# A layer of attention and MLP on one core: a constant by memset, and magnitudes of weights as sums on ScalarE

## The chip, the core and the metric

The kernel runs on one core of a Trainium2 chip. The core has TensorE (PE, with its weight loads as PEld), VectorE (DVE), ScalarE (ACT), GpSimd (POOL) and SyncE (SP), which here issues all transfers. Each engine works through its own instructions in a fixed order and waits where a semaphore isn't yet up, so whatever stands behind a waiting instruction waits too. The metric is device time in microseconds for one execution; lower is better.

## The reference

For x of 2048 rows by 512, with 32 heads of 16 and an MLP of width 1792:

```python
xn = _layernorm(x)
qkv = (xn @ wqkv)                         # wqkv 512 x 1536
scores = einsum("bhqd,bhkd->bhqk", q, k) * 16 ** -0.5
o = einsum("bhqk,bhkd->bhqd", softmax(scores), v)
A = o @ wo                                # wo 512 x 512
h = gelu(xn @ w1 + b1)                    # w1 512 x 1792, tanh form
B = h @ w2 + b2                           # w2 1792 x 512
return x + A + B
```

## The kernel before, in words

**Numbers in two halves.** TensorE works in 16-bit floats. Each operand is split into a high and a low half, and a product is the sum of three (high by high, high by low, low by high). Weights are divided first by a power of two near their magnitude, so that the halves keep their range. That magnitude is measured on the chip: `absmax` (L728) reduces a chunk of weights to one value per partition on VectorE, and `scales` (L123) turns the values into one power of two per tensor by a transposition, a maximum, a product that spreads it to all partitions, and a mask on the bits. `fac` is the power, `inv` its inverse. `gs` (L954) holds four factors made from them.

**Stages.** 1. A prelude: `stats` normalises the rows of x, four tiles of 128 rows at a time (a block; the second half of each later block on ScalarE, in two passes over `xs`, L783 and L784), `transpose_x` transposes them to `xt`, `project` computes q and k of the first eight heads, `v_proj` computes v for one tile of 128 rows. q and k go through DRAM (`qk_d`) and come back as *stacks* (`kst`, `qst`): for a pair of heads 128 partitions, of which 48 per head hold the halves, two more rows per head hold the row maxima on the q side against a constant 1024 (`MROW`) on the k side, and the others hold zero. 2. The loop of `unit`s: 512 units for eight groups of four heads, each unit with scores for four heads (`s_half`, row maxima `mt` by VectorE at L260), exponentials of an earlier unit (`e_half`, ScalarE at L305), products with v (`v_half`) and a share of other matrix products on the same TensorE order (`dense`): first the projections of the remaining heads, then the MLP, then the output projection. 3. A tail.

In the prelude `tile_and_unit` runs four times per block: one tile of v beside the first sixteen units' scores. Their maxima are taken by VectorE as in the loop.

**The weights of the MLP.** `measure` (L829) goes over 16 chunks of 128 x 1024 values of w1, w2 and wo, each in two halves; `MEASURE` (L33) says how many halves follow each tile of the prelude: 0, 1 and 2 in blocks 1 to 3, 3 in the last four units. That is 24 halves; the other 8 are taken in the loop, one per unit, where `prepare` (L962) begins with `yield from ms`. Then `prepare` computes the factors and splits the chunks, which are loaded a second time (`every` holds the list twice), on GpSimd, in steps that are paid out at 2500 ns a unit. Chunks stand in three buffers named `wch`.

**The constant of the stacks.** `clear` (L82) sets each of the 32 stacks to zero on GpSimd and copies two rows of 1024 into each k stack per head by a transfer of 2 KB from `ones_row`, 16 transfers for each of the two sets: L88, 32 in all.

**Order.** Up to L1015 a scheduler chooses the order on each engine by its own estimates of times, so a change in one place can move many instructions of the prelude. From L1015 on (`manual_schedule`) the order is that of the code.

Of the kernel before, what the change touches and what calls it, by code (L numbers as in the profile page):

```python
# [1 line left out]

# [6 lines left out]
F32 = mybir.dt.float32  # L9
F16 = mybir.dt.float16  # L10
I32 = mybir.dt.int32
AF = mybir.ActivationFunctionType
ALU = mybir.AluOpType
AX = mybir.AxisListType
# [3 lines left out]
P = 128  # L18
# [11 lines left out]
VW = DH + 1  # L30
LEAD = 19
FAST, MEAN, SLOW = (4, 4), (3, 4), (3, 3)
MEASURE = (3, 0, 1, 2)  # L33
HALF = 1300
POOL_NS = 2500
TAIL = 5
# [4 lines left out]
GELU_C = 0.7978845608028654  # L41
GELU_A = 0.044715
MROW = 1024.0
W = 2 * P


@with_exitstack
def layer_kernel(ctx: ExitStack, tc: tile.TileContext, x, wqkv, wo, w1, b1, w2, b2, out):
    nc = tc.nc
# [3 lines left out]
    def pool(stack, name, bufs=1, space=None, side=None):  # L53
# [3 lines left out]
    const = pool(ctx, "const")  # L57
    work = pool(ctx, "work")
# [13 lines left out]

    ident = const.tile([P, P], F32, name="ident")
    make_identity(nc, ident)
    ones_row = const.tile([2, P], F16, name="ones_row")
    nc.vector.memset(ones_row, MROW)


    kst, qst = ([[[const.tile([P, QB], F16, name=f"{x}st{i}_{p}_{b}") for b in range(NQB)] for p in range(2)]
                 for i in range(2)] for x in "kq")  # L80

    def clear(i):  # L82
        for b in range(NQB):
            for p in range(2):
                for st in (kst[i][p][b], qst[i][p][b]):
                    nc.gpsimd.memset(st.bitcast(F32), 0.0)
                for a in range(2):
                    nc.sync.dma_start(kst[i][p][b][64 * a + 62:64 * a + 64, :].rearrange("r (b n) -> r b n", n=P),  # L88
                                      ones_row.unsqueeze(1).to_broadcast([2, 4, P]))

    vv = const.tile([P, NT, H * VW + 15], F32, name="vv")
    nc.gpsimd.memset(vv[:, :, 0:H * VW].rearrange("p t (h e) -> p t h e", e=VW)[:, :, :, DH], 1.0)
# [66 lines left out]
    def given(engine, ns):  # L159
        backlog[engine] += ns  # L160
# [102 lines left out]
    def s_end(u):  # L263
# [10 lines left out]
        def store():  # L274
# [433 lines left out]
    with ExitStack() as st1:  # L708
# [10 lines left out]
        def chunk(src):  # L719
            wf = ph.tile([P, 4 * W], F32, name="wch", bufs=3)  # L720
            v = wf.rearrange("p (a b) -> p a b", b=src.shape[2])
# [6 lines left out]
        def absmax(dst, v):  # L728
            nc.vector.tensor_reduce(dst, v, axis=AX.XY if len(v.shape) == 3 else AX.X, op=ALU.max,  # L729
                                    apply_absolute_value=True)  # L730
            given("dve", 600)
# [4 lines left out]
        wov = wo.rearrange("(c p) n -> p c n", p=P)  # L736
        every = [w1v[:, :, i * W:(i + 1) * W] for i in range(7)]
        every = every + [w2v[:, 2 * i:2 * i + 2, :] for i in range(7)] + [wov[:, 0:2, :], wov[:, 2:4, :]]
        every = every + every
        amx = work.tile([P, 16, 2], F32, name="amx")  # L740
        fac1 = []

        def fetch(k):
# [10 lines left out]
        loads = []  # L754
        wvf = [chunk(wvv[:, :, i * W:(i + 1) * W]) for i in range(2)]
        wvh = [ph.tile([P, NC, D], F16, name="wvh", tag="wsp", bufs=3) for _ in range(2)]
        fac_v, ready_w = [], {}
# [53 lines left out]
        def prep_v():  # L811
# [9 lines left out]
            for i in range(2):  # L821
                cs = slice(i * W, (i + 1) * W)
                split(wvh[0][:, :, cs], wvh[1][:, :, cs], wvf[i], inv[:, 0:1])

        def some(gen, n):
            for _ in range(n):
                next(gen, None)

        def measure():  # L829

            for n in range(16):
                v = fetch(n)
                for k in range(2):
                    absmax(amx[:, n, k:k + 1], v[:, 2 * k:2 * k + 2, :] if n < 7 else v[:, k, :])
                    yield

        ms = measure()

# [57 lines left out]
        for sb in range(1, NQB):  # L896
# [15 lines left out]
            for j in range(4):  # L912
                tile_and_unit(4 * sb - 4 + j)
                some(ms, MEASURE[sb])
                if sb == 1:
# [7 lines left out]
        for j in range(4):  # L923
            some(pq, 2)
            tile_and_unit(NT - 4 + j)
            some(ms, MEASURE[0])
        run(pq)
# [26 lines left out]
        gs = const.tile([P, 4], F32, name="gs")  # L954
# [6 lines left out]

        def prepare():  # L962
            yield from ms
            am = work.tile([P, 10], F32, name="am_all")
            nc.vector.tensor_reduce(am[:, 0:7], amx[:, 0:7, :], axis=AX.X, op=ALU.max)
            nc.vector.tensor_reduce(am[:, 7:8], b1_s, axis=AX.X, op=ALU.max, apply_absolute_value=True)
            nc.vector.tensor_reduce(am[:, 8:9], amx[:, 7:14, :], axis=AX.XY, op=ALU.max)
            nc.vector.tensor_reduce(am[:, 9:10], amx[:, 14:16, :], axis=AX.XY, op=ALU.max)
            box = []
            yield  # L970
            yield from scales(am, 10, sbank, box)
            inv, fac = box
            fac1.append(fac)

            nc.vector.reduce_max(gs[:, 0:1], fac[:, 0:8], axis=AX.X)
            nc.vector.tensor_tensor(gs[:, 3:4], fac_v[0][:, 0:1], fac[:, 9:10], op=ALU.mult)
            yield
            nc.vector.reciprocal(gs[:, 1:2], gs[:, 0:1])
            nc.vector.tensor_tensor(gs[:, 2:3], gs[:, 0:1], fac[:, 8:9], op=ALU.mult)
            yield  # L980
            nc.vector.tensor_scalar_mul(gs[:, 1:2], gs[:, 1:2], 0.5)
            ended = [True]
            for n in range(16):
                v = fetch(16 + n)
                while not ended[0]:
                    yield
                ended[0] = False

                def then(wh=None, n=n):
                    ended[0] = True  # L990
                    later(2, lambda: put(wh, n), True)
# [256 lines left out]
```

## Time and profile before

| What | Value |
|---|---|
| median of 3 runs | 1513.81 us (1510.95 to 1516.05) |
| profiled execution | 1513.79 us, its span 1512.0 us |
| busy: TensorE, VectorE, ScalarE, GpSimd | 1489.9, 1405.0, 1244.0, 663.7 us |
| prelude: first products of q and k; second block of x transposed from | 15.97 us; 23.65 us |
| prelude: first four units' v products; next four; third block's projection | 31.82 to 47.81 us; 56.75 to 71.96 us; to 77.8 us |
| table load on ScalarE, first exponentials | 120.56 us, 1.28 us long |
| last unit's scores | about 1450 us |

A row of the profile's groups reads: line, engine, operation, tile written <- tiles read, shape, count, then busy time and mean ns of one, then idle time before it and what ended that. A row of a timeline begins with start and length in us, and ends with the count of merged instructions and, in brackets, the idle time before and its releaser. A row of windows gives a stretch, its length, busy time and count of each engine, the granted TensorE clock, the share of the transfer engines and GB/s. The matmuls' ends are modelled, so TensorE can read as fully busy while its products are spaced apart.

### The profile page before, as it was taken

How to read it: one execution, taken by the hardware profiler on the slowest of the kernel's cores; microseconds unless marked ns; L12 is line 12 of the kernel's file. 1: busy time of each engine (PE TensorE's matmuls, PEld its weight loads, DVE VectorE, ACT ScalarE, POOL GpSimd, SP SyncE). 2: the span in 40 equal slices, each digit the busy share in tenths (PEclk: the TensorE clock that was granted, in tenths of full speed). 3: DMA queues.
4: the chain of work that ended last, by engine and by line, in shares of the span. 5: the costliest groups of instructions: out<-in, count | busy, mean ns of one | idle time of the engine just before them, and what ended most of it. 6: DMA issues, size and time to landing. Idle time of an engine off the chain costs nothing.

```text
span 1512.0 us, 86779 instructions
## 1 busy us (share of the span) xinstructions
PE 1489.9 (99%) x39407; PEld 822.7 (54%) x39407; DVE 1405.0 (93%) x2368; ACT 1244.0 (82%) x2317; POOL 663.7 (44%) x685
## 2 busy tenths in 40 slices
PE   8999999999999999999999999999999999999998
PEld 4434555555555555555555555555555555555553
DVE  7899999999999999999999999999999999999933
ACT  4326788889998888999888899998889998888885
POOL 4113598637772111777411158761216785211110
PEclk9999999999999999999999999999999999999998
DMA  6454477632222201131011211122102201112422
GB/s 199 132 160 148 148 218 228 195 106 81 67 78 57 70 27 35 44 84 50 22 50 42 65 41 43 36 78 64 34 18 62 79 27 29 49 54 60 131 65 97
DMA packets 113673, 123.75 MB, mean 82 GB/s; under 512 B 24988, under 2 KB 85276, under 8 KB 113304
## 3 DMA queue, kind: packets, MB, share of 16 engines
q1 hardware_dynamic: 113304, 118.21, 25.9%
q8 instruction: 308, 5.05, 1.4%
q14 instruction: 61, 0.50, 0.1%
HBM read 80.61 MB, written 37.34 MB: 78 GB/s over the span
## 4 chain that ended last, share of the span: by engine, by line
PE 81%; DVE 16%; issue 1%; DMA 1%; ACT 1%; POOL 0%; SPq 0%; ACTq 0%; POOLq 0%
PE pV L169 24%; PE pD L169 20%; PE pT L169 17%; PE pS L169 17%; DVE mt L260 14%; PE pT L438 1%; PE pD L438 1%; DVE amx L729 1%; PE pT L531 1%; PE pV L531 0%; DMA wq<-in_A_wqkv_dram 0%; DMA wch<-in_B_w_dram 0%; PE pT L799 0%; PE pS L438 0%; POOL xt L804 0%
## 5 line engine op out<-in xcount | busy, mean ns | idle before, releaser
L260 DVE TENSOR_REDUCE mt<-pS 128x1 f32<-128x512 f32 x2048 | 1304.7, 684 | 41.8 <-PE pS L169 25.9
L305 ACT ACTIVATE pe<-pT 128x512 f32<-128x512 f32 x2048 | 1112.3, 598 | 172.4 <-PE pS L169 82.0
L169 PE MATMUL pV<-pe,vv 64*32 64x512 f32 x8192 | 1076.5, 595 | 0.1
L169 PE MATMUL pT<-qst,kst 64*32 64x512 f16 x8192 | 719.5, 378 | 1.4 <-ACT pe L305 1.2
L169 PE MATMUL pS<-kst,qst 62*32 62x512 f16 x8192 | 624.8, 379 | 6.4 <-DVE mt L260 4.9
L169 PEld LDWEIGHTS <-kst 64*32 64x32 f16 x8192 | 289.4, 91 | 191.8 <-issue 94.2
L169 PEld LDWEIGHTS <-qst 62*32 62x32 f16 x8192 | 274.3, 92 | 206.0 <-issue 60.6
L169 PE MATMUL pD<-w_s,g 64*32 64x512 f16 x5376 | 364.6, 376 | 0.0
L169 PE MATMUL pD<-xb,wc 64*32 64x512 f16 x5376 | 361.1, 377 | 0.0
L169 PEld LDWEIGHTS pV<-pe,vv 64*32 64x32 f32 x8192 | 181.5, 105 | 88.4 <-PE pV L169 4.7
L1090 POOL TENSOR_TENSOR xa<-xa,yt 128x512 f32<-128x512 f32 x16 | 20.5, 1279 | 302.9 <-ACT yt L1088 302.9
L169 PEld LDWEIGHTS <-wc 64*32 64x32 f16 x5376 | 117.0, 91 | 42.7 <-issue 0.5
L169 PEld LDWEIGHTS <-g 64*32 64x32 f16 x5376 | 112.3, 91 | 45.6
L169 PE MATMUL pD<-xt,wqk_h 64*32 64x512 f16 x2016 | 135.9, 380 | 0.6 <-issue 0.4
L361 POOL TENSOR_TENSOR osb<-osb,rb 128x512 f32<-128x512 f32 x31 | 39.9, 1286 | 158.9 <-DMA rb<-den_d 120.3
L1045 POOL TENSOR_TENSOR t<-hh 128x512 f32<-128x512 f32 x56 | 58.3, 1041 | 86.5 <-ACT hh L1065 85.4
L1047 POOL TENSOR_TENSOR t<-t,hh 128x512 f32<-128x512 f32 x56 | 71.9, 1285 | 4.7
L1040 POOL TENSOR_TENSOR t<-t,hh 128x512 f32<-128x512 f32 x56 | 71.9, 1283 | 4.7
L1042 POOL TENSOR_TENSOR g<-t,g 128x512 f16<-128x512 f32 x56 | 65.2, 1165 | 4.7
L1039 POOL TENSOR_SCALAR t<-t,gs 128x512 f32<-128x512 f32 x56 | 39.0, 696 | 49.7 <-ACT t L1034 49.3
L169 PEld LDWEIGHTS <-wqk_h 64*32 64x32 f16 x2016 | 48.5, 92 | 21.5 <-issue 5.4
L169 PE MATMUL pD<-wo_s,oc 64*32 64x512 f16 x828 | 54.5, 378 | 0.0
(141 smaller groups left out, 868.9 us busy)
## 6 DMA issues: line engine op xcount, KB each, us to landing
wch<-in_B_w_dram SPq DMA_DIRECT2D x28, 512.0 KB
wc<-w_d SPq DMA_DIRECT2D x56, 256.0 KB
qk_d<-stg SPq DMA_DIRECT2D x32, 256.0 KB
rb<-den_d SPq DMA_DIRECT2D x124, 64.0 KB
w_d<-wsp SPq DMA_DIRECT2D x28, 256.0 KB
kst<-qk_d SPq DMA_DIRECT2D x128, 48.0 KB
qst<-qk_d SPq DMA_DIRECT2D x128, 48.0 KB
xs<-in_A_x_dram SPq DMA_DIRECT2D x16, 256.0 KB
```

The lines of the kernel that those rows point to most:

```text
L169: p = nc.tensor.matmul(*args, **kw)
L260: nc.vector.reduce_max(mt_of[t][:, n, qt, kb:kb + 1], s, axis=AX.X)
L305: nc.scalar.activation(pe, st, AF.Exp, scale=scale_of[g // 2])
L361: pooled((1280, lambda: nc.gpsimd.tensor_tensor(osb, osb, rb, op=ALU.mult)), (620, lambda: nc.gpsimd.tensor_scalar(ot[:, 0], osb, 1.0, 0.0 ...
L438: nc.tensor.matmul(self.bank, lhs, rhs, start=start, stop=self.last and self.over())
L531: nc.tensor.matmul(pj, xt[:, i, c, t * P:(t + 1) * P], wh[j][:, c, :], start=(n == 0), stop=(n == 11))
L1039: pooled((690, lambda: nc.gpsimd.tensor_scalar(t1, t1, 1.0, gs[:, 1:2], op0=ALU.add, op1=ALU.mult)), (1280, lambda: nc.gpsimd.tensor_tenso ...
L1040: (1280, lambda: nc.gpsimd.tensor_tensor(t1, t1, hh, op=ALU.mult)),
L1042: (1160, lambda: nc.gpsimd.tensor_tensor(g[:, 1, f, :], t1, g[:, 0, f, :], op=ALU.subtract)),
L1045: pooled((1040, lambda: nc.gpsimd.tensor_tensor(t1, hh, hh, op=ALU.mult)), (620, lambda: nc.gpsimd.tensor_scalar(t1, t1, 1.0, 1.0 / GELU_A ...
L1047: (1280, lambda: nc.gpsimd.tensor_tensor(t1, t1, hh, op=ALU.mult)),
L1090: add = lambda: nc.gpsimd.tensor_tensor(xa, xa, yt, op=ALU.add)
```

## The change

Three things change. `clear` fills each k stack with a 32-bit word that holds the 16-bit float 1024 twice, by one memset, and makes no transfers; the unused rows of k now hold 1024 and meet zeros on the q side. `measure` takes each chunk whole, by one pass of ScalarE that writes absolute values over the chunk, scaled by 1/32, and sums them to one value per partition; the sum of 1024 magnitudes over 32 stands in for the largest magnitude. `MEASURE` puts one such pass behind each tile of blocks 2 and 3 and two behind each of the last four, sixteen in all, so none is left for the loop. Two one-column multiplications of `gs` go from VectorE to GpSimd.

```diff
-MEASURE = (3, 0, 1, 2)
+MEASURE = (2, 0, 1, 1)
+MROWS = struct.unpack("f", struct.pack("ee", MROW, MROW))[0]
+SPREAD = 32.0
...
-                for st in (kst[i][p][b], qst[i][p][b]):
-                    nc.gpsimd.memset(st.bitcast(F32), 0.0)
-                for a in range(2):
-                    nc.sync.dma_start(kst[i][p][b][64 * a + 62:64 * a + 64, :].rearrange("r (b n) -> r b n", n=P),
-                                      ones_row.unsqueeze(1).to_broadcast([2, 4, P]))
+                nc.gpsimd.memset(kst[i][p][b].bitcast(F32), MROWS)
+                nc.gpsimd.memset(qst[i][p][b].bitcast(F32), 0.0)
...
-                for k in range(2):
-                    absmax(amx[:, n, k:k + 1], v[:, 2 * k:2 * k + 2, :] if n < 7 else v[:, k, :])
-                    yield
+                dst = am_all[:, n:n + 1] if n < 7 else amx[:, n:n + 1]
+                nc.scalar.activation(v, v, AF.Abs, scale=1.0 / SPREAD, accum_out=dst)
+                yield
...
-            nc.vector.tensor_reduce(am[:, 0:7], amx[:, 0:7, :], axis=AX.X, op=ALU.max)
...
-            nc.vector.tensor_tensor(gs[:, 3:4], fac_v[0][:, 0:1], fac[:, 9:10], op=ALU.mult)
+            nc.gpsimd.tensor_tensor(gs[:, 3:4], fac_v[0][:, 0:1], fac[:, 9:10], op=ALU.mult)
...
-            nc.vector.tensor_tensor(gs[:, 2:3], gs[:, 0:1], fac[:, 8:9], op=ALU.mult)
+            nc.gpsimd.tensor_tensor(gs[:, 2:3], gs[:, 0:1], fac[:, 8:9], op=ALU.mult)
```

The scheduler's order in the prelude moves with it. Line numbers of the changed kernel are up to two lower than before, below its import also one higher. ScalarE, at the second block of x, before (`stg` is the eviction of q and k, `sd` a square root of variances, `xt` the copies of the transposed block):

```order
L501 ACTIVATE stg<-pS 128x512
L768 ACTIVATE sd<-sd 128x4
L783 ACTIVATE xs<-xs,sd 128x512 x2
L501 ACTIVATE stg<-pS 128x512
L784 ACTIVATE xs<-xs,sd 128x512 x2
L800 ACTIVATE xt<-pT 128x512
```

and in the changed kernel at the same place:

```order
L499 ACTIVATE stg<-pS 128x512
L767 ACTIVATE sd<-sd 128x4
L782 ACTIVATE xs<-xs,sd 128x512 x2
L833 ACTIVATE wch,am_all<-wch 128x1024
L783 ACTIVATE xs<-xs,sd 128x512 x2
L499 ACTIVATE stg<-pS 128x512
L799 ACTIVATE xt<-pT 128x512
```

The first Abs pass stands between the two passes over `xs`, and the second eviction of `stg` has moved behind them.

SyncE's transfers at that place, before, from the last two of the constant's transfers on:

```order
L88 DMA kst_1_3_88<-ones_row 2x4x128 x2
L717 DMA xs<-in_A_x_dram 128x512 x4
L495 DMA qk_d<-stg 128x2x512
L496 DMA qk_d<-stg 128x512
L495 DMA qk_d<-stg 128x2x512
L496 DMA qk_d<-stg 128x512
L717 DMA xs<-in_A_x_dram 128x512
L404 DMA kst_0_0_81<-qk_d 48x512 x2
```

and in the changed kernel:

```order
L715 DMA xs<-in_A_x_dram 128x512 x4
L454 DMA wq<-in_A_wqkv_dram 128x4x128 x2
L721 DMA wch<-in_B_w_dram 128x4x256
L494 DMA qk_d<-stg 128x512
L927 DMA b_s<-in_B_b_dram 128x14x1
L493 DMA qk_d<-stg 128x2x512
L721 DMA wch<-in_B_w_dram 128x4x256
L402 DMA kst_0_0_79<-qk_d 48x512
L494 DMA qk_d<-stg 128x512
```

The next weights `wq`, two chunks and the bias `b_s` have come ahead of the first read of a stack; the second chunk's buffer is free when the first Abs pass is done.

VectorE in the first units of the loop, before:

```order
L462 TENSOR_REDUCE am_qk<-wq 128x1
L729 TENSOR_REDUCE amx<-wch 128x1
L260 TENSOR_REDUCE mt<-pS 128x1 x4
L128 TENSOR_REDUCE sc_r<-pS 2x1
L729 TENSOR_REDUCE amx<-wch 128x1
L260 TENSOR_REDUCE mt<-pS 128x1 x4
L133 TENSOR_SCALAR sc_c<-pS 128x2
```

and in the changed kernel, with the ten magnitudes' `sc_r` where `amx` stood:

```order
L460 TENSOR_REDUCE am_qk<-wq 128x1
L126 TENSOR_REDUCE sc_r<-pS 10x1
L258 TENSOR_REDUCE mt<-pS 128x1 x4
L460 TENSOR_REDUCE am_qk<-wq 128x1
L131 TENSOR_SCALAR sc_c<-pS 128x10
L258 TENSOR_REDUCE mt<-pS 128x1 x4
L126 TENSOR_REDUCE sc_r<-pS 2x1
```

No pass over a chunk is left between the maxima, and the steps of `prepare` stand eight units earlier.

More of the change, by code (lines that the diff above doesn't have):

```diff
@@ L1 @@
+import struct
 from contextlib import ExitStack
@@ L74, in layer_kernel @@
     make_identity(nc, ident)
-    ones_row = const.tile([2, P], F16, name="ones_row")
-    nc.vector.memset(ones_row, MROW)
     kst, qst = ([[[const.tile([P, QB], F16, name=f"{x}st{i}_{p}_{b}") for b in range(NQB)] for p in range(2)]
@@ L739, in layer_kernel @@
         every = every + every
-        amx = work.tile([P, 16, 2], F32, name="amx")
+        amx = work.tile([P, 16], F32, name="amx")
+        am_all = work.tile([P, 10], F32, name="am_all")
         fac1 = []
@@ L963, in prepare @@
             yield from ms
-            am = work.tile([P, 10], F32, name="am_all")
-            nc.vector.tensor_reduce(am[:, 0:7], amx[:, 0:7, :], axis=AX.X, op=ALU.max)
+            am = am_all
             nc.vector.tensor_reduce(am[:, 7:8], b1_s, axis=AX.X, op=ALU.max, apply_absolute_value=True)
-            nc.vector.tensor_reduce(am[:, 8:9], amx[:, 7:14, :], axis=AX.XY, op=ALU.max)
-            nc.vector.tensor_reduce(am[:, 9:10], amx[:, 14:16, :], axis=AX.XY, op=ALU.max)
+            nc.vector.tensor_reduce(am[:, 8:9], amx[:, 7:14], axis=AX.X, op=ALU.max)
+            nc.vector.tensor_reduce(am[:, 9:10], amx[:, 14:16], axis=AX.X, op=ALU.max)
             box = []
```

## The prediction

> **What bounds the kernel now.** I read the page first, then the chain that ended last, then windows and the timelines of the first 165 us.
>
> ```profile
> span 1512.0 us, 86779 instructions
> PE 1489.9 (99%) x39407; PEld 822.7 (54%) x39407; DVE 1405.0 (93%) x2368; ACT 1244.0 (82%) x2317; POOL 663.7 (44%) x685
> PE 81%; DVE 16%; issue 1%; DMA 1%; ACT 1%; POOL 0%; SPq 0%; ACTq 0%; POOLq 0%
> ```
>
> The profiled execution has a span of 1512.0 us and took 1513.79 us, 0.02 us under the median of the runs (1513.81), so differences worked out on its span carry over to the median. TensorE is busy 99% of it, and the chain is 81% TensorE and 16% VectorE (almost all of that the row maxima `mt`). So only what shortens TensorE's waits or its stretched passages can pay. VectorE's passes are the second bound: in the main loop four maxima stand in every unit.
>
> ```profile
> 120.00:130.00 10.00, 5.52 (x9) 0.83 0.62 197
> 130.00:140.00 10.00, 8.21 (x15) 1.00 0.44 129
> 140.00:150.00 10.00, 8.97 (x15) 1.00 0.25 81
> 150.00:160.00 10.00, 7.00 (x12) 1.00 0.13 43
> 500.00:700.00 200.00, 193.18 (x309) 1.00 0.17 49
> ```
>
> These rows are windows of the maxima alone (busy time, count). In the settled loop 309 pass in 200 us, 0.647 us each or 2.59 us a unit. In 130 to 160 us only 42 pass in 30 us, and in 120 to 130 only 9. That is where the removed work on VectorE hurts.
>
> **The change part by part.** *1. The 32 halves of `absmax` leave VectorE.*
>
> ```profile
> L729 DVE TENSOR_REDUCE amx<-wch 128x1 f32<-128x512 f32 x32 | 21.1, 674 | 0.9 <-DMA wch<-in_B_w_dram 0.9
> 119.90 0.60 DVE amx L729
> 129.00 0.58 DVE amx L729
> 82.33 1.28 DVE L260 TENSOR_REDUCE mt<-pS 128x1 f32<-128x512 f32 x2
> 83.52 0.68 DVE L729 TENSOR_REDUCE amx<-wch 128x1 f32<-128x512 f32 x1
> 84.11 1.28 DVE L260 TENSOR_REDUCE mt<-pS 128x1 f32<-128x512 f32 x2
> 79.44 0.41 PE L169 MATMUL pS<-kst,qst 62*32 62x512 f16 x8
> 79.78 1.47 PE L531 MATMUL pV<-wvh,xt 128*128 128x512 f16 x6
> 91.19 0.40 PE L169 MATMUL pS<-kst,qst 62*32 62x512 f16 x4 [0.65 <-DVE mt L260]
> ```
>
> The group is 32 x 0.674 = 21.1 us busy; back to back one takes 0.59 us, as the chain (second and third row) shows. They count only where TensorE waits for VectorE. Between 78 and 108 us it nearly doesn't: a half unit on VectorE takes 84.11 - 82.33 = 1.78 us (two maxima and one `amx`), on TensorE 0.34 us for the eight score pieces (79.78 - 79.44) and 1.40 for six projection products. Sixteen half units give 16 x (1.78 - 1.74) = 0.6 us, the hole at 91.19 gives 0.65, and I add 0.25 for lesser ones: -1.5 us (bounds 0 and -3). In the loop from 120 us the maxima set the pace. With `amx` gone and the pace at 0.647, the 42 maxima of 130 to 160 us need 27.2 us instead of 30: -2.8. Of the slow 120 to 130 us I count only the two `amx` that stand on the chain, 2 x 0.6: -1.2, because the rest there is the table load of ScalarE and a halved clock (below). That part is bounded by 0 and by the full pace, 10 - 9 x 0.647 = 4.2.
>
> *2. Two multiplications of `gs` go to GpSimd.*
>
> ```profile
> 152.52 0.99 DVE L976 TENSOR_TENSOR gs<-fac,fac 128x1 f32<-128x1 f32 x1
> 155.89 2.07 DVE L979 TENSOR_TENSOR gs<-gs,fac 128x1 f32<-128x1 f32 x1
> 158.62 0.40 PE L169 MATMUL pS<-kst,qst 62*32 62x512 f16 x4 [1.63 <-DVE mt L260]
> ```
>
> They took 0.99 and 2.07 us for one element a partition, and TensorE's wait of 1.63 us stands right behind the second. They are inside the 2.8 us above and are not counted again. On GpSimd they stand between splits of `wq`, ahead of nothing that is needed within 20 us.
>
> *3. Sixteen Abs passes of 128x1024 enter ScalarE's order.* No row shows an Abs with a sum. The nearest is the split of `wvh`:
>
> ```profile
> xs<-in_A_x_dram SPq DMA_DIRECT2D x16, 256.0 KB
> 22.88 1.33 ACT L784 ACTIVATE xs<-xs,sd 128x512 f32<-128x512 f32 x2
> 27.57 2.23 ACT L145 ACTIVATE wvh<-wch,inv 128x1024 f16<-128x1024 f32 x2
> 15.97 6.15 PE L438 MATMUL pS<-xt,wqk_h 128*128 128x512 f16 x24
> 23.65 0.33 PE L799 MATMUL pT<-ident,xs 128*128 128x128 f32 x1
> 31.82 2.75 PE L531 MATMUL pV<-wvh,xt 128*128 128x512 f16 x12
> 38.39 0.40 PE L169 MATMUL pS<-kst,qst 62*32 62x512 f16 x4
> 38.72 0.39 PE L531 MATMUL pT<-wvh,xt 128*128 128x512 f16 x1
> 47.81 0.55 PE L799 MATMUL pT<-ident,xs 128*128 128x128 f32 x3
> 0.00:10.00 10.00, 6.76 (x22) 2.39 (x22) 5.73 (x15) 1.49 (x2) 7.27 (x31) 1.00 0.78 250
> 22.00:25.00 3.00, 2.12 (x16) 1.69 (x16) 2.82 (x12) 2.24 (x4) 0.00 (x0) 1.00 0.68 203
> 25.00:28.00 3.00, 2.32 (x14) 1.15 (x13) 1.49 (x3) 3.00 (x7) 1.35 (x2) 1.00 0.92 330
> ```
>
> Two passes of 1024 took 2.23 us, so I take 1.1 us; bounds 1.1 (that row) and 2.4 (twice the row and a little, if the sum cost a second pass). [...]
>
> The first Abs is the expensive one. It stands in ScalarE's order between the two steps that normalise `xs` (L783, L784); the second began at 22.88. Its chunk of 512 KB is issued behind four `xs` and two `wq` of 256 KB each: 2.1 MB together, from about 15.9 us, when the last transpose of the first block (just ahead of the products at 15.97) releases the `xs` buffers. At the 250 GB/s of 0 to 10 us (start included) that is 8.4 us, landing at 24.3. Abs ends at 25.4 instead of L784 beginning at 22.88: everything that ScalarE feeds, and so the transposes at 23.65, comes 2.5 us later. With the 330 GB/s of 25 to 28 us it would be 0.5, with the 203 of 22 to 25 us 4.4. I take the row that also begins with an empty queue: +2.5.
>
> That is mostly won back by TensorE's new order. Before, sixteen score groups of four stand alone at 0.33 us each (38.72 - 38.39), 5.3 us; now fourteen of them stand in pairs at 0.34, two alone: 7 x 0.34 + 2 x 0.33 = 3.0. So -2.2. The block that ran from 31.82 to 47.81 then runs from about 34.3 to 48.
>
> Later Abs passes bunch: eleven stand in the second block of four units, 56 to 77 us, beside some 12 passes of 512, 0.67 us each as L784's pair shows: 11 x 1.1 + 12 x 0.67 = 20 us in 21. They just fit, but at the end of the block the last copies of `xt` wait for two of them: +0.3 (bounds 0 and +3). The other five lie in waits of ScalarE, at nothing; without that cover they would cost 1.1 us each.
>
> *4. The 32 transfers of the constant go; one memset per stack stays.*
>
> ```profile
> 8.17 12.63 SPq L88 DMA_DIRECT2D kst<-ones_row  x16
> 20.91 2.27 SPq L717 DMA_DIRECT2D xs<-in_A_x_dram  x4
> 28.31 2.49 SPq L404 DMA_DIRECT2D kst<-qk_d  x4
> 43.06 10.66 SPq L88 DMA_DIRECT2D kst<-ones_row  x16
> L86 POOL MEMSET kst<- 128x256 f32 x16 | 5.1, 320 | 0.0
> ```
>
> SyncE loses 12.6 and 10.7 us of issue. The next `xs` start at 15.9 instead of 20.91, but TensorE was not waiting for those tiles, and the first read of a stack, at 28.31, waits for `qk_d` to land. In the new order it stands behind a chunk that waits for the first Abs (25.4), and the bias `b_s` lies between the two writes of `qk_d`. I take its time as unchanged: 0 (bounds -1 and +3). The memset writes the same bytes, so its 320 ns stay.
>
> *5. The steps of `prepare` come eight units earlier*, since all sixteen Abs stand ahead of the loop. The splits on GpSimd start earlier and end earlier; projections, not splits, end that phase: 0 (bounds -1 and +1).
>
> Sum: -1.5 - 2.8 - 1.2 + 2.5 - 2.2 + 0.3 = -4.9 us; 1513.8 - 4.9 = 1508.9 us, 0.32% less. A measurement of this kernel tells about 0.3%, 4.5 us, from no change, so the forecast lies just outside.
>
> **The rivals.** *A. The new gap halves the clock.*
>
> ```profile
> 11.00:17.00 6.00, 4.93 (x21) 3.94 (x21) 5.73 (x19) 3.01 (x6) 2.33 (x4) 0.50 0.42 134
> 121.00:124.00 3.00, 1.90 (x34) 0.66 (x40) 1.98 (x5) 2.91 (x5) 1.04 (x1) 0.91 0.80 277
> 124.00:126.00 2.00, 2.00 (x40) 0.77 (x29) 1.97 (x4) 1.08 (x2) 0.00 (x0) 0.50 0.16 45
> ```
>
> After the idle start the granted clock was 0.50 for 6 us; after 1.90 busy of 3 us at 121 to 124 it fell to 0.50 again. At 22 to 28 us (rows above), with 2.12 and 2.32 busy of 3, it stayed at 1.00. With the first Abs late, TensorE has from 22.1 to about 26 us only a few small products. If the clock halves for some 5 us of dense work, 2.6 us are lost: 1511.5 us, within 0.3%. [...] Chance 0.22.
>
> *B. Slower: Abs with a sum costs two passes.* Place: ScalarE, 56 to 77 us. With 2.4 us the eleven passes and the rest take 11 x 2.4 + 8 = 34 us in 21; the evictions, the copies of `xt` and the projection behind them come 13 us late: 1522 us. From 1.2 us a pass (13 us over 11) it begins to cost, from 1.6 it eats the gain. Against it: a 1024-wide pass of ScalarE shows 1.1 us. Chance 0.17, with other late transfers in front of ScalarE that would give as much.
>
> *C. More is won.* If the first chunk lands by 22.3 and 120 to 130 us comes near the settled pace, 1.9 and 2 us more go: 1505 us. Chance 0.15.
>
> *D. The work is hidden anyway:* TensorE is 99% busy, only 16% of the chain are VectorE's. But the 42 maxima in 30 us are a rate, and a rate can't be hidden. This leaves perhaps half the gain, 1511 us; I count it with A and the upper edge of the forecast.
>
> **How the numbers follow.** Forecast 0.45, in its own range of 1506.5 to 1511 (0.36 of it beyond 0.3%, 0.09 within). A 0.22, C 0.15, B 0.18 with its neighbours. Faster by over 0.3%: 0.36 + 0.15 = 0.51; within: 0.09 + 0.22 = 0.31; slower: 0.18. The range leaves out the upper part of B and the lower tail of C: 1503.5 to 1516.5 us.
>
> **What would show it.** Right: the settled pace of maxima from 130 us on; no TensorE wait behind `gs`; Abs passes of about 1.1 us; the first transposes of the second block near 26 us, and the block after them ending near 48. Wrong: an Abs over 1.3 us; stacks read later than 31 us; a clock of 0.50 between 24 and 32 us; or a second block of units that ends after 78 us. The prediction fails as a whole if the loop after 120 us keeps 2.8 us a unit without `amx`: then something other than VectorE sets that pace.

## The result: no difference, because gains of some 7 us meet losses of about that size

The changed kernel took 1515.78 us (median, 1513.91 to 1519.23) beside 1515.37 us for the kernel before (1510.95 to 1522.63): a ratio of 1.0001, 95% interval 0.9992 to 1.0011. The page of the changed kernel, span, TensorE's row and the head of the chain:

```profile
span 1513.5 us, 86739 instructions
PE 1487.6 (98%) x39407; PEld 818.9 (54%) x39407; DVE 1385.3 (92%) x2332; ACT 1259.7 (83%) x2349; POOL 662.7 (44%) x687
PE 84%; DVE 13%; issue 2%; ACT 1%; DMA 1%; POOL 0%; SPq 0%; ACTq 0%; POOLq 0%
```

TensorE is busy 2.3 us less than before in a span 1.5 us longer. VectorE's share of the chain fell from 16 to 13%, so the work that was taken off VectorE did leave the path. The windows of the running maxima (length, busy time, count, granted clock) show it directly:

```profile
120.00:130.00 10.00, 7.31 (x12) 1.00 0.43 133
130.00:140.00 10.00, 8.76 (x14) 1.00 0.59 183
140.00:150.00 10.00, 9.63 (x16) 1.00 0.69 217
150.00:160.00 10.00, 9.09 (x15) 1.00 0.43 125
```

45 maxima pass in 130 to 160 us, where 42 did, and 12 instead of 9 in 120 to 130 us, where the clock now stays at 1.00. The loop began later, though: ScalarE loads its table for the exponentials at 123.47 us instead of 120.56. Cut at four events, the two executions compare like this. (The first projection is the matmul group that began at 15.97 us before; it ended at 22.12 and 21.98 us.) Stretches are compared here, because the time up to that event varies between executions of the same instructions: it is 22.1 us before, with a granted clock of 0.50 at 12 to 16 us, and 20.6 and 20.7 us in two runs below whose prelude is the same (the products alone; more data), with a clock of 1.00 there.

| Stretch | before | changed | difference |
|---|---|---|---|
| start to the end of the first projection | 22.1 us | 22.0 us | -0.1 |
| from there to the third block's first scores (77.70, 82.91) | 55.6 | 60.9 | +5.3 |
| from there to the table load (120.56, 123.47) | 42.9 | 40.6 | -2.3 |
| from there to the end | 1391.4 | 1390.0 | -1.4 |

The loss of 5.3 us happens at 67 to 83 us. First TensorE's timeline in the third projection, before and changed (start, length; in brackets the wait and who ended it):

```profile
74.59 0.59 PE L438 MATMUL pD<-xt,wqk_h 128*128 128x512 f16 x2 [0.30 <-POOL xt L804]
75.02 2.75 PE L438 MATMUL pT<-xt,wqk_h 128*128 128x512 f16 x12
```

```profile
76.83 0.38 PE L436 MATMUL pD<-xt,wqk_h 128*128 128x512 f16 x1 [2.91 <-ACT xt L799]
...
78.55 0.59 PE L436 MATMUL pD<-xt,wqk_h 128*128 128x512 f16 x2 [0.91 <-POOL xt L803]
78.98 4.01 PE L436 MATMUL pT<-xt,wqk_h 128*128 128x512 f16 x10
```

Both begin the third projection at about 71.9 us (71.96 and 71.81). The changed kernel then waits 2.91 us for a copy `xt` of ScalarE and 0.91 us for the low half that GpSimd makes from a copy `pf`; and behind these gaps ten products take 4.01 us, where twelve took 2.75: the granted clock fell to 0.50, as the window of the changed kernel shows (the clock stands third from the end):

```profile
80.00:82.00 2.00, 2.00 (x6) 0.74 (x5) 0.69 (x1) 0.35 (x1) 0.00 (x0) 0.50 0.19 66
```

(2.91 + 0.91 - 0.30) for the waits and 4.01 - 10 x 0.229 = 1.7 for the clock make 5.2 us. What ScalarE did meanwhile, the copy before and then the changed kernel:

```profile
72.22 0.59 ACT L800 ACTIVATE xt<-pT 128x512 f16<-128x512 f32 x1
```

```profile
67.69 1.06 ACT L833 ACTIVATE wch<-wch 128x1024 f32<-128x1024 f32 x1 [2.38 <-DMA wch<-in_B_w_dram]
...
71.88 1.06 ACT L833 ACTIVATE wch<-wch 128x1024 f32<-128x1024 f32 x1 [0.72 <-DMA wch<-in_B_w_dram]
73.21 1.06 ACT L833 ACTIVATE wch<-wch 128x1024 f32<-128x1024 f32 x1 [0.17 <-DMA wch<-in_B_w_dram]
74.66 1.06 ACT L833 ACTIVATE wch<-wch 128x1024 f32<-128x1024 f32 x1 [0.30 <-DMA wch<-in_B_w_dram]
75.72 0.58 ACT L532 ACTIVATE vv<-pT 128x512 f32<-128x512 f32 x1
76.19 0.59 ACT L799 ACTIVATE xt<-pT 128x512 f16<-128x512 f32 x1
76.67 0.60 ACT L802 ACTIVATE pf<-pT 128x512 f32<-128x512 f32 x1
```

L833 is the pass of absolute values. Five of them stand between 67 and 76 us (one at 69.04 is left out here), and each waits first for its own chunk to land (2.38, 0.20, 0.72, 0.17 and 0.30 us). The copies that TensorE waits for stand behind them: ScalarE could have made `xt` once TensorE's transposes were through, at about 72 us (before, it made it at 72.22), and made it at 76.19.

The second loss is in the loop. TensorE's idle time from 180 to 290 us was 0.9 us before and is 4.1 us now, and the view of waits names nobody for it:

```profile
PE pV L167 <- issue: 1.6, 1, 1.6
PE pD L167 <- issue: 1.4, 2, 0.8
PE pT L167 <- issue: 1.1, 1, 1.1
```

Over the whole program the kernel before has 0.4 us of this kind. Without the 3.2 us of additional idle time the last stretch of the table would have gained 4.6 us instead of 1.4. So in these two profiles gains of 2.3 and 4.6 us meet losses of 5.3 and 3.2; that leaves the changed kernel 1.5 us longer, while the medians lie 0.4 us apart.

The four stops end at 202.76, 230.02, 239.94 and 246.69 us, each in the middle of a group of matmuls that needs nothing new:

```profile
246.69 0.61 PE L167 MATMUL pV<-pe,vv 64*32 64x512 f32 x1 [1.56 <-issue]
```

The page's list of queues and the view of transfers of the changed kernel, here for 244 to 245 us, show what comes at these places:

```profile
q8 instruction: 308, 5.05, 1.4%
```

```profile
q8 instruction: 1, 0.02, 6.0%
```

308 packets of 16.4 KB for 2 x 39407 matmuls and weight loads make 256 instructions to a packet, so these are taken for the blocks of TensorE's own program. One takes 6.0% of 16 engines x 1 us = 0.96 us. The packets ahead of the four stops begin at 200.48, 227.62, 237.59 and 244.33 us and end at 201.44, 228.55, 238.55 and 245.29; TensorE goes on 1.32, 1.47, 1.39 and 1.39 us after each. This distance is what speaks for late instructions: the profiles of this case, all kernels taken together, hold 46 stops of TensorE without a named releaser, and every one ends 1.22 to 1.50 us after the end of such a packet. So TensorE is taken to have run out of instructions there, though no row names it. How far the packets lie apart doesn't tell a stop by itself: those before the four stops start 5.6 to 6.7 us after the one before, but in the kernel before, where the median in the loop is 4.5 us, 24 packets come over 5.4 us after the last and only one of them is followed by a stop.

### The profile page after: what moved, and what is told of

It is laid out like the page before. It is cut to its first block, busy times and chain, and to the rows that moved or that the text cites. A ratio compares the mean times of both kernels' runs of the same rounds, so it can differ in the third digit from the quotient of the medians.

```text
span 1513.5 us, 86739 instructions
## 1 busy us (share of the span) xinstructions
PE 1487.6 (98%) x39407; PEld 818.9 (54%) x39407; DVE 1385.3 (92%) x2332; ACT 1259.7 (83%) x2349; POOL 662.7 (44%) x687
## 4 chain that ended last, share of the span: by engine, by line
PE 84%; DVE 13%; issue 2%; ACT 1%; DMA 1%; POOL 0%; SPq 0%; ACTq 0%; POOLq 0%
PE pV L167 24%; PE pD L167 21%; PE pT L167 18%; PE pS L167 17%; DVE mt L258 11%; PE pT L529 1%; PE pT L436 1%; PE pV L529 1%; PE pD L436 1%; DVE bs L762 0%; DMA wch<-in_B_w_dram 0%; DMA xs<-in_A_x_dram 0%; PE pT L798 0%; PE pS L436 0%; POOL xt L803 0%
## 5 line engine op out<-in xcount | busy, mean ns | idle before, releaser
L258 DVE TENSOR_REDUCE mt<-pS 128x1 f32<-128x512 f32 x2048 | 1305.7, 684 | 55.4 <-PE pS L167 37.6
L167 PE MATMUL pS<-kst,qst 62*32 62x512 f16 x8192 | 616.7, 378 | 2.7 <-DVE mt L258 1.5
L167 PEld LDWEIGHTS <-wc 64*32 64x32 f16 x5376 | 116.9, 91 | 42.9 <-issue 0.7
```

The lines of the kernel that those rows point to most:

```text
L167: p = nc.tensor.matmul(*args, **kw)
L258: nc.vector.reduce_max(mt_of[t][:, n, qt, kb:kb + 1], s, axis=AX.X)
```

## Each part by itself

Theory P: the passes stand in ScalarE's order ahead of copies that TensorE needs, and wait there for transfers; the parts themselves are good. Theory F: the stops in the loop are late instruction blocks. The rivals are in the expectations.

**The memset alone**, with the maxima left on VectorE:

```diff
-                for st in (kst[i][p][b], qst[i][p][b]):
-                    nc.gpsimd.memset(st.bitcast(F32), 0.0)
-                for a in range(2):
-                    nc.sync.dma_start(kst[i][p][b][64 * a + 62:64 * a + 64, :]...
...
+                nc.gpsimd.memset(kst[i][p][b].bitcast(F32), MROWS)
+                nc.gpsimd.memset(qst[i][p][b].bitcast(F32), 0.0)
```

> The key stacks' constant by memset alone; the maxima stay on VectorE. Theory P (placement: the change lost 5.2 us at 67 to 83 us, because passes of absolute values stood in ScalarE's order ahead of the copies that TensorE needed, and waited for their transfers): there are no such passes here, so nothing waits at 67 to 83 us; the loop begins (the first score matmuls of the running units) between 117 and 120 us against 119.31 before, the maxima in the loop stay, and the time is 1513 to 1516 us, at most 2 us under the kernel before. Rival M (taking the 32 transfers away is itself what costs, because it lets the weights' chunks crowd the queue 20 us earlier): the loop begins at 122 us or later, as in the changed kernel, and the time is 1517 us or more.

Measured 1512.38 us, 0.9989 of before (0.9979 to 0.9999). The loop begins at 116.82 us, 3.7 us earlier; 1.7 of these lie ahead of the end of the first projection, where executions differ anyway, so 2.0 are left. The rest is 1.3 us longer. Rival M falls: the transfers' absence doesn't cost. What it does is pull the weights' chunks ahead. The windows of the maxima `amx`, before and with the memset alone:

```profile
20.00:56.00 36.00, 0.00 (x0) 1.00 0.44 141
56.00:76.00 20.00, 3.76 (x6) 1.00 0.66 192
```

```profile
20.00:56.00 36.00, 7.24 (x11) 1.00 0.68 199
56.00:76.00 20.00, 8.24 (x14) 1.00 0.68 208
```

25 of the 32 now run before 76 us, where 6 did. On VectorE this costs nothing (from the first projection to the third block it takes 55.4 us, as before), and with none of them left from 76 to 98 us the stretch of the sixteen half units takes 41.0 us instead of 42.9.

**The absolute values and the products, with the 32 transfers put back:**

```diff
-                nc.gpsimd.memset(kst[i][p][b].bitcast(F32), MROWS)
-                nc.gpsimd.memset(qst[i][p][b].bitcast(F32), 0.0)
+                for st in (kst[i][p][b], qst[i][p][b]):
+                    nc.gpsimd.memset(st.bitcast(F32), 0.0)
+                for a in range(2):
+                    nc.sync.dma_start(kst[i][p][b][64 * a + 62:64 * a + 64, :]...
```

> The sums of absolute values and the two products on GpSimd, with the 32 transfers put back. The transfers of the second 16 constants stand ahead of the weights' chunks again, so the first pass of absolute values cannot come before about 66 us. Theory P: all but one pass stand behind the last copy of the fourth block's transposes, the loop begins at 117.5 to 120 us (before 119.31, changed kernel 122.93), keeps the 6 us that the changed kernel gained in it from 120 to 160 us, and the time is 1507 to 1512 us: 1507 to 1509 if TensorE does not stop for instruction blocks at 200 to 247 us as in the changed kernel, 1511 to 1512 if it does (theory F). Rival R (the passes on ScalarE cost wherever they stand): the loop begins at 122 us or later and the time is 1514 us or more.

Measured 1506.48 us, 0.9949 (0.9936 to 0.9962). Its profile has 4.2 us of stops without a named releaser, and it is still 4.5 us under what was expected with them. Here is ScalarE where the fourth block's copies are made:

```profile
66.14 1.05 ACT L838 ACTIVATE wch<-wch 128x1024 f32<-128x1024 f32 x1
...
67.18 0.59 ACT L804 ACTIVATE xt<-pV 128x512 f16<-128x512 f32 x1
...
70.06 0.59 ACT L804 ACTIVATE xt<-pT 128x512 f16<-128x512 f32 x1
...
71.01 1.07 ACT L838 ACTIVATE wch<-wch 128x1024 f32<-128x1024 f32 x1
```

One pass stands ahead of the copies, and none waits: the 16 transfers of the second set hold back the chunks, so it seems that the scheduler has no pass to put forward. Thus the memset gives 0.9989 alone, the other two parts give 0.9949 alone, and all three together give 1.0001. What one part freed, the next one filled at the wrong place.

**The products alone:**

```diff
-            nc.vector.tensor_tensor(gs[:, 3:4], fac_v[0][:, 0:1], fac[:, 9:10], op=ALU.mult)
+            nc.gpsimd.tensor_tensor(gs[:, 3:4], fac_v[0][:, 0:1], fac[:, 9:10], op=ALU.mult)
...
-            nc.vector.tensor_tensor(gs[:, 2:3], gs[:, 0:1], fac[:, 8:9], op=ALU.mult)
+            nc.gpsimd.tensor_tensor(gs[:, 2:3], gs[:, 0:1], fac[:, 8:9], op=ALU.mult)
```

> Only the two one-element products go from VectorE to GpSimd; all else as before. If the wait of TensorE behind them (1.63 us) was paid once and not made up: 1.0 to 2.0 us faster than before, 1513.5 to 1514.5. If VectorE's next maximum was late anyway because of the maxima of the weights around it: within 0.5 us of before.

Measured 1510.86 us, 0.9975 (0.9964 to 0.9987): 3.8 us, more than either case. In its profile TensorE idles 1.9 us from 120 to 160 us instead of 3.7, and 0.4 us from 180 to 290 instead of 0.9. From the table load to the end it takes 1388.8 us instead of 1391.4; from the first projection to the table load it takes 0.6 us more, with the same instructions as before, which shows how far two executions differ. So the profiles place 2.0 to 2.6 us of the 3.8, near the small end of the interval.

**The memset and the products together**, the maxima on VectorE:

> The memset of the constant and the two products on GpSimd, with the maxima left on VectorE. The parts alone measured 0.9989 and 0.9975 of before; if they add: 0.9964, 1509.3 us. Against it the run with the passes held back (1505.7) then shows what the magnitudes on ScalarE are worth by themselves when they stand nowhere in the way: 3 to 4 us, all of it in the loop from 117 to 160 us, where the maxima stand among the running maxima of the scores. If it comes to 1507 us or less, the magnitudes on ScalarE are worth at most 1 us.

Measured 1510.64 us, 0.9969 (0.9958 to 0.9980). The parts nearly add (0.9964). It has 3.2 us of stops without a named releaser, so stops come without the passes of ScalarE too.

**The products back on VectorE in the changed kernel** (the diff of the products in reverse):

> The changed kernel with the two one-element products back on VectorE. If they cost there what they cost with the maxima on VectorE (the two alone measured 0.9975 of before, 3.8 us): 1518 to 1520 us. If only TensorE's wait of 1.63 us behind them counts: 1516.5 to 1518. If the maxima around them were what made them dear: 1515 to 1516.5, no difference.

Measured 1512.76 us, 0.9986 (0.9972 to 1.0000). This lies below all three ranges: on VectorE the products are no dearer here, if anything cheaper than in the changed kernel. A product on VectorE and the pass on GpSimd beside it, with the memset alone, then both products and the pass beside the second in this run:

```profile
150.68 2.06 DVE L976 TENSOR_TENSOR gs<-gs,fac 128x1 f32<-128x1 f32 x1
```

```profile
150.59 2.13 POOL L956 TENSOR_TENSOR wsp<-wch,wsp 128x1024 f16<-128x1024 f32 x1
```

```profile
129.09 0.14 DVE L974 TENSOR_TENSOR gs<-fac,fac 128x1 f32<-128x1 f32 x1
...
131.62 0.24 DVE L977 TENSOR_TENSOR gs<-gs,fac 128x1 f32<-128x1 f32 x1
```

```profile
130.68 1.16 POOL L150 TENSOR_TENSOR wqk_h<-wq,wqk_h 128x512 f16<-128x512 f32 x1
```

The product of one element ends with GpSimd's two-tensor pass: 150.68 + 2.06 = 152.74 and 150.59 + 2.13 = 152.72. The other product of that run took 0.98 us and ended at 148.29, a pass of GpSimd at 148.28. In the later run the first finds GpSimd between passes (0.14 us), the second meets the last 0.2 us of one that ends at 131.84 (0.24 us). So their price was neither the products' own nor that of the maxima around them, but where they fell. Why a product lasts until such a pass ends, the profiles don't show.

## The passes held back

In the changed kernel each pass gets a bias column of zeros that GpSimd makes from a value tile, so that no pass can be ordered ahead of that tile:

```diff
+        zc = work.tile([P, 16], F32, name="zc")
...
-                nc.scalar.activation(v, v, AF.Abs, scale=1.0 / SPREAD, accum_out=dst)
+                t = n if n < 4 else 8 + (n - 4) * 2 // 3
+                nc.gpsimd.tensor_scalar(zc[:, n:n + 1], vv[:, t, 0:1], 0.0, 0.0, op0=ALU.mult, op1=ALU.add)
+                nc.scalar.activation(v, v, AF.Abs, scale=1.0 / SPREAD, bias=zc[:, n:n + 1], accum_out=dst)
```

> The changed kernel with each pass of absolute values held back until a value tile is ready: the first four to value tiles 0 to 3, the other twelve to tiles 8 to 15 (from about 83 us), by a bias column of zeros that GpSimd makes from that tile. No pass stands ahead of the fourth block's copies. Theory P: TensorE does not wait at 74 to 79 us, the third projection ends at 77 to 78.5 us (before 77.7, changed kernel 82.9), the loop begins at 117 to 119 us, and the time is 1509 to 1512 us; 4 us less again, 1505 to 1508, if the late instruction blocks of 200 to 247 us do not come (theory F). If the fall at 67 to 83 us has another cause (the clock after the gap at 22 us, the transfers themselves): the third projection still ends at 81 us or later and the time is 1514 us or more.

Measured 1505.74 us, 0.9940 (0.9927 to 0.9953). TensorE at the third projection, and ScalarE where twelve of the passes now stand:

```profile
73.61 0.59 PE L436 MATMUL pD<-xt,wqk_h 128*128 128x512 f16 x2 [0.30 <-POOL xt L804]
74.04 2.75 PE L436 MATMUL pT<-xt,wqk_h 128*128 128x512 f16 x12
```

```profile
81.22 1.15 ACT L836 ACTIVATE wch<-wch,zc 128x1024 f32<-128x1024 f32 x1 [0.31 <-POOL zc L835]
...
82.36 1.13 ACT L836 ACTIVATE wch<-wch,zc 128x1024 f32<-128x1024 f32 x1
...
83.79 0.60 ACT L532 ACTIVATE vv<-pT 128x512 f32<-128x512 f32 x1 [0.20 <-PE pT L529]
```

The waits of 2.91 and 0.91 us and the slow products are gone; the projection ends at 76.7 us, the loop begins at 117.23 and the stretch from the first projection to the third block takes 56.3 us instead of 60.9. In the later blocks ScalarE has nearly 2.9 us free between copies (one ends at 80.91 us, the next begins at 83.79), so the same passes (1.13 to 1.15 us each with the bias column) are hidden there. This settles P: the passes cost by their place. The holding back moves the chunks' transfers too, but the transfers by themselves don't cost it: with the memset alone 14 half chunks are taken at 56 to 76 us, at 208 GB/s (231 in the changed kernel), and TensorE loses nothing there. The time came out 3 us below the range given for a run with stops (it has 1.8 us of them), so the gain of the loop had been put too low. It is 4.9 us under the memset and the products together (1510.64 us): so much are the magnitudes worth on ScalarE when they stand out of the way, where 3 to 4 had been expected.

Is it the passes' length, or their waits? **A quarter of the columns**, everything else kept but for a few neighbours in the order:

```diff
-                nc.scalar.activation(v, v, AF.Abs, scale=1.0 / SPREAD, accum_out=dst)
+                q = v[:, 0, 0:256]
+                nc.scalar.activation(q, q, AF.Abs, scale=1.0 / SPREAD, accum_out=dst)
```

> The changed kernel with each pass over 256 of the 1024 columns of its chunk alone (three quarters of the magnitudes are left out); the transfers, the buffers and nearly the whole order of ScalarE are as in the changed kernel. It parts the two halves of theory P. If the waits for transfers in ScalarE's order are what delay the copies: the third projection still ends at 80.5 us or later (changed kernel 82.9, before 77.7), the time is 1513 to 1516 us. If the passes' own 1.25 us each are: it ends at 77 to 79 us, and the time is 1508 to 1511 us.

Measured 1513.22 us, 0.9991 (0.9977 to 1.0006), and the third projection ends at 84.5 us: both as given for the waits. ScalarE ahead of the late copy:

```profile
73.83 0.42 ACT L834 ACTIVATE wch<-wch 128x256 f32<-128x256 f32 x1 [1.04 <-DMA wch<-in_B_w_dram]
...
75.17 0.42 ACT L834 ACTIVATE wch<-wch 128x256 f32<-128x256 f32 x1 [0.84 <-DMA wch<-in_B_w_dram]
...
76.48 0.42 ACT L834 ACTIVATE wch<-wch 128x256 f32<-128x256 f32 x1 [0.80 <-DMA wch<-in_A_wo_dram]
...
77.37 0.59 ACT L799 ACTIVATE xt<-pT 128x512 f16<-128x512 f32 x1
```

The passes shrank from 1.06 to 0.42 us, and their waits grew to 1.04, 0.84 and 0.80: a pass starts every 1.3 us whatever its length. That is the pace of the chunks: 512 KB in 1.34 us is 390 GB/s, and two of the busiest windows of 2 us in the changed kernel, from 66 and from 76 us, show 401 and 364. The projection began late in this run (74.09 us instead of 71.81), so its length says more than its end: it takes 10.4 us, 11.1 in the changed kernel and 5.7 before, and TensorE waits 1.82 and 1.34 us in it. It is the waits, then: a pass of less than half the length helps by 0.7 us, a pass that stands elsewhere by the rest.

## The stops in the loop

**Fewer data in the stretch**: twelve of the sixteen stores `xn_d` put off in the changed kernel.

```diff
-                later(10 + 3 * k, lambda c=c, cols=cols: nc.sync.dma_start(xn_d[:, :, c, cols], ...
+                later((10 if k < 4 else 50) + 3 * k, lambda c=c, cols=cols: nc.sync.dma_start(xn_d[:, :, c, cols], ...
```

> The changed kernel with twelve of the sixteen 256 KB stores of the normalized rows (xn_d) put off by 40 slots, from about 170-272 us to 280-380 us, where the transfers are few. Theory F (TensorE stops at 202, 229, 239 and 245 us because the blocks of its own instructions come late behind data transfers): with a quarter less data in 180 to 250 us the stops shrink or go: TensorE's idle time in 180 to 280 us falls from 4.1 us to under 2, and the time by 2 to 4 us, to 1512 to 1514. The 5 us lost at 67 to 83 us stay. If the stops have to do with something else (POOL's splits, the order of SP's queue): idle time in 180 to 280 us stays at 3.5 us or more and the time within 1 us of the changed kernel's 1515.8.

Measured 1519.21 us, 1.0035 (1.0021 to 1.0049). The idle time did fall, from 4.1 to 1.4 us in 180 to 290 us. But the gain was paid back, and more: what is still in the list of put-off stores when the projections end is issued at once, eight stores at 310.9 to 317.6 us, and the first weights of the feed-forward part queue behind them:

```profile
PE pT L167 <- ACT hh L1063: 4.2, 1, 4.2
```

`hh` is the first eviction of that part; ScalarE made it after a wait of 4.87 us for its weights `wc`. The two together, -2.7 and +4.2 us, are 1.5 of the 3.4 us by which the median is longer; the profile doesn't place the rest. Put off together with the passes held back, the same happens:

> The passes held back (as in the run with the bias column) and the twelve stores put off together. Theory P and F: what both gain, as the idle time of TensorE in 180 to 290 us is 2.9 us with the passes held back: 1503 to 1505 us, against 1505.7 with the passes held back alone. If the stops do not hang on the data: 1505 to 1507 us, with 2.5 us idle or more left.

Measured 1513.22 us, 0.9992 (0.9981 to 1.0003), 7.5 us over the run with the passes held back alone; the wait for `hh` is 5.1 us. The milder form, only the last eight stores, `10 + 3 * k if k < 8 else 44 + 2 * (k - 8)`, all out before that part:

> The passes held back, and only the last eight stores of the normalized rows put off, by at most 20 slots, so that four of them go from 207-242 us to behind 247 us and all are out by 285 us, before the feed-forward part reads them back at 291 us. Theory F: less data at 207 to 247 us, so TensorE's idle time at 180 to 290 us falls from 2.9 us to 1 to 2 us, and the time from 1505.7 to 1504 to 1505 us. If the stores only move the stops: 1505.5 to 1507 us.

Measured 1504.67 us, 0.9929 (0.9908 to 0.9949). That can't be told from the 0.9940 without it. Its profile has 4.0 us idle in 180 to 290 us, not 1 to 2; but the execution profiled is the slowest of the six (1510.45 us), so it says little of the median. As far as it goes, this run speaks against a simple rule by the amount of data.

**More data**, in the kernel before:

```diff
+    more_d = dram.tile([16, P, 4, W], F32, name="more_d")
...
+            for k in range(16):
+                later(90 + 2 * k if k < 8 else 135, lambda k=k: nc.sync.dma_start(more_d[k], w1v[:, :, k % 7 * W:(k % 7 + 1) * W]), True)
```

> The kernel before with sixteen extra transfers of 512 KB, device memory to device memory, that nothing waits for: eight of them one per two slots from about 350 us (some 5 us apart), and eight all at once at about 475 us, both in stretches where TensorE had no idle time to speak of (0.2 us in 20) and the transfers a share of 0.2 to 0.3. Theory F: the eight at once hold the queues for over 10 us; in that time an instruction block comes late, and TensorE stops one to three times for 1 to 6 us in all, each time ending 1.2 to 1.5 us after the end of an instruction packet; the spread ones cost under 1 us. The time is 2 to 7 us over before. If instruction blocks pass the data: no stop without a named releaser, and at most the waits for stacks that come late.

Measured 1541.48 us, 1.0164 (1.0143 to 1.0185), far over the range. As with the stores, the list was emptied when the projections ended, so all sixteen came in one row, and what spread transfers cost was not tested. SyncE, then TensorE's waits and timeline:

```profile
314.99 22.83 SPq L937 DMA_DIRECT2D more_d<-in_B_w_dram  x16
```

```profile
PE pD L170 <- DMA wc<-w_d: 11.8, 1, 11.8
```

```profile
326.50 0.39 PE L170 MATMUL pT<-qst,kst 64*32 64x512 f16 x3 [2.17 <-issue]
...
334.06 1.04 PE L170 MATMUL pV<-pe,vv 64*32 64x512 f32 x3 [0.75 <-issue]
```

Of the 27 us, 16.2 are TensorE's waits for `wc` (11.8) and for `qst` (4.4), data that queued behind the extra ones. But two stops have no data to wait for, 2.17 and 0.75 us in a stretch that had none in the kernel before. The instruction packets, which come 3.8 to 5.1 us apart at 350 to 400 us of the kernel before, begin at 316.06, 324.12 and 331.76 us; the last two end at 325.08 and 332.64, and TensorE goes on 1.42 us after each. So with the transfer engines full (data alone are 98.5% of them from 324 to 325 us and 100.8% from 331 to 333) the packets came 8.1 and 7.6 us apart, and TensorE stopped: shown, by these two stops. How much a given schedule loses by it is not predicted by the sum of data. In 180 to 290 us the transfers have a share of 0.71 in the kernel before and of 0.74 with the products alone, with 0.4 and 0.3 us of stops, and of 0.62 in the changed kernel with its 4.1; why is open. Each kernel was profiled in one execution, so it is not known either how much the stops of one kernel vary.

## Why the prediction was wrong

It forecast 1508.9 us and -4.9, with a loss of 2.5 for a late first pass; it measured no difference. Point by point:

- *Point 1, the prelude, -1.5.* Measured -2.3 (42.9 to 40.6 us), within the bounds. The half units do run at 1.74 us. But the reason was not quite the one given: with the maxima left on VectorE and the memset alone the stretch is 41.0 us, because the maxima had moved ahead of it.
- *Point 1, the loop, -2.8 and -1.2.* The maxima reach 45 in 130 to 160 us and 12 in 120 to 130; with the passes held back 48 and 13. From the table load to the end 5.1 us were gained with the passes held back (1386.3 us, 1.8 of it stops), 1.4 in the changed kernel with its 4.1 us of stops. The rate argument was right and somewhat low; the loop was then stopped for another reason, which the prediction didn't have.
- *Point 2, the products.* TensorE's wait behind them is gone, as said. In the changed kernel that part gives nothing, since in their earlier place the products were cheap on VectorE too (0.14 and 0.24 us).
- *Point 3, the first pass, +2.5.* Wrong: its chunk landed at 22.5 us, not 24.3, because the `xs` were issued from 13.15 us and not from 15.9; the 2.1 MB came at 224 GB/s, where 250 had been taken. The second step over `xs` began at 23.59 instead of 22.88, 0.7 us later:

```profile
22.53 1.06 ACT L833 ACTIVATE wch<-wch 128x1024 f32<-128x1024 f32 x1 [0.97 <-DMA wch<-in_B_w_dram]
23.49 0.19 ACT L833 ACTIVATION_READ_ACCUMULATOR wch<-wch 128x1 f32 x1
23.59 1.32 ACT L783 ACTIVATE xs<-xs,sd 128x512 f32<-128x512 f32 x2
```

  The block of units behind it began 1.6 us later (33.43 instead of 31.82); part of that is the clock, under rival A.

- *Point 3, the pairs, -2.2.* The block that took 15.99 us (31.82 to 47.81) took 14.59 (33.43 to 48.02): -1.4. It ended near 48, as said, though partly by luck: the late start and the pairs' gain were both put too high by about as much.
- *Point 3, the passes in the second block.* **This is the step that failed**: "They just fit, but at the end of the block the last copies of `xt` wait for two of them: +0.3 (bounds 0 and +3)." The step added up ScalarE's busy time (11 x 1.1 + 12 x 0.67 = 20 us in 21). A pass did take 1.04 us from start to start where its chunk was there (57.46 to 58.50 us), no more than the 1.1 taken. But its chunk had to land first: the last three passes ahead of the late copy start 1.33 and 1.45 us apart, and the first of the five waits 2.38 us. The 4.9 us that ScalarE waited for chunks in 60 to 80 us were not in the sum. Together with the drop of the clock behind them they made the third projection 11.1 us long instead of 5.7 (71.81 to 82.91, before 71.96 to 77.70). So this one term is +5.4, out of its bounds, and alone turns -4.9 into no difference.
- *Point 4, the constant, 0 (-1 and +3).* Alone -1.6 us (0.9989), a bit beyond, though the interval reaches back into them. Its real effect was on the order: it moved all sixteen chunks ahead, and with them the passes.
- *Point 5, prepare earlier, 0.* The stops don't need it: they also come, 3.2 us, where prepare has its late place (the memset and the products together).
- *Rival A, the clock halves in the new gap.* It did in the profiled execution. The windows of the changed kernel:

```profile
24.00:26.00 2.00, 1.78 (x9) 1.78 (x10) 2.00 (x6) 1.55 (x4) 0.00 (x0) 0.61 0.54 131
26.00:28.00 2.00, 2.00 (x10) 1.45 (x8) 0.80 (x2) 1.96 (x5) 0.36 (x1) 0.53 1.07 344
```

  The drop to 0.61 and 0.53 at 24 to 28 us cost about 0.7 us, an estimate from two other runs: from the product that follows the first projection to the first scores there are 9.0 us with the memset alone, where the clock stays at 1.00 after a wait of 1.7 us, and 9.7 us with the passes held back, where it is 0.50 from 24 to 26 us after a wait of the same length. That is a quarter of the 2.6 us given. The drop came behind waits of 1.03 and 0.93 us in a row. As the wait of 1.7 us was followed by 1.00 in one run and by 0.50 in the other, the length of a wait alone doesn't tell; what else decides is open.
- *Rival B, two passes per Abs.* Its place and its victims were right (ScalarE at 56 to 77 us, the copies of `xt` and the projection), its cause was wrong: a sum shows as an extra instruction of 0.19 us that overlaps the next pass, and lateness came from transfers, which the text named only in passing ("with other late transfers in front of ScalarE").

The sign that was set for a failure came true: the second block of units and the projection behind it ended at 82.9, after 78 us.

## What to carry to other kernels

Before giving an idle engine work that has to wait for a transfer, look at what stands behind it in that engine's order: the copies behind ScalarE's passes here stood still through its waits for chunks as well (4.9 us in 60 to 80 us), and a sum of durations didn't see that. Where a scheduler sets the order, parts of a change need not add (0.9989 and 0.9949 alone, 1.0001 together); freeing a queue can move the next part's work to where it hurts, so give such work a dependence that names its place. Here a bias column made from a later tile turned no difference into 0.6% less time.

## What was not expected of the hardware

Packets of 16.4 KB in the queue of kind `instruction`, 308 in one execution, came over the same 16 transfer engines as the data, one about every 4.5 us of this loop (median 4.47 us before, 4.53 in the changed kernel); by their number they are taken for TensorE's program in blocks of 256 instructions. In the 46 stops without a named releaser that the profiles of this case hold, TensorE stood still for 0.2 to 2.2 us, until 1.22 to 1.50 us after the end of such a packet. With the transfer engines full of the extra data, two packets came 8.1 and 7.6 us after the one before, and TensorE stopped for 2.17 and 0.75 us. And a one-element product on VectorE took 0.14 us beside an idle GpSimd and up to 2.07 us; with the memset alone the two of 0.98 and 2.06 us ended with passes of GpSimd over two tensors (148.29 us beside 148.28, 152.74 beside 152.72).
